# Second MLP of a fused attention and two-MLP kernel: early token sums kept in program order, three plain token quarters split ahead and sent through DRAM

## The chip, the cores and the metric

One core of one Trainium2 chip. The metric is the device time of one execution in microseconds, the median of three runs. Engines are named as the profile names them: PE (TensorE matmul), PEld (its weight load), DVE (VectorE), ACT (ScalarE), POOL (GpSimd), SP (SyncE, whose queue issues all the DMAs of this kernel).

## What is computed

Attention through 32 packed tokens per head, then a gated MLP with an RMS norm, then a second MLP. The change lies in the second MLP alone:

```python
def _moe2_ref(x, w_in, w_out):          # x: 4608 x 512, w_in: 512 x 2048, w_out: 2048 x 512
    h = x @ w_in
    g = h * (1.0 / (1.0 + np.exp(-1.702 * h)))
    return (g @ w_out).astype(np.float32)
```

## The kernel before

Every matrix product is made of three matmuls: an operand is split into a high part (a rounded copy, `fp32r`) and a low part (the value less its high part), and high*high, high*low and low*high are added in PSUM. A split is therefore always a copy on ACT and a subtraction on DVE or POOL.

The second MLP (`mlp2`, `main` in it) multiplies 2x2 blocks with seven products in place of eight. The tokens go through it in five batches, the list `spans`: three of 2 x 512 tokens, two of 2 x 384. The four quarters of a batch's activations are `b11`, `b12`, `b21`, `b22` (half of the tokens by half of the 512 columns; 128 partitions x 2 x 512, or x 2 x 384), and the seven operands that multiply are three plain quarters, `b11`, `b21`, `b22`, and four sums: t1 = b12 - b11, t3 = b22 - b12, t2 = b22 - t1, t4 = b21 - t2. Each lives, split, in one tile of its own (`x_tile`, `x_b...` and `x_t...` in the profile), which the next batch overwrites.

A batch takes four groups of hidden columns (`NGR`), each of 14 up products (`up`, L1065 in the profile: six matmuls; two rounds a = 0, 1 of the seven operands). Beside the ups of one group run the seven down products (`down`, L1136: 24 matmuls of 256 columns, or 18) of the group before, one down after two ups. `form` (L1101 to L1110) makes the down operands: sums on DVE, `oh` on ACT, `ol` on POOL. Weights come from DRAM in the order of use: `wi`, `WIB` ups ahead, `wo`, four downs ahead.

The next batch's quarters are loaded by `load_x` into `xr` tiles (three in the tag `raw`, one in `xr`). `sums` forms t1, t3, t2 in the third and fourth group (table `EARLY`: steps counted from the third group's first up; L1024, L1026, L1030), and after the last use of an operand, in the last seven ups, `prepare` splits the new one into its tile (L1041 on ACT; L1042 on POOL for the plain quarters, on DVE for the sums) and forms t4 (L1045). Nothing ties the early sums to a place: Tile's scheduler orders each engine's instructions by its own estimate of when they are ready, unless `tc.keep_in_program_order` pins one behind what is already written for its engine. An engine runs its instructions in that order, and so does the SP queue.

The four table entries and lines that matter:

```python
EARLY = {10: "t1", 13: "t3", 16: "t2"}            # and load_x at step 6
nc.vector.tensor_sub(xr[q], xr["b12"], xr["b11"])          # sums, t1
(nc.gpsimd if q[0] == "b" else nc.vector).tensor_sub(...)  # prepare, low part
nc.gpsimd.tensor_sub(ol, src, fl(oh))                      # form
```

Of the kernel before, what the change touches and what calls it, by code (L numbers as in the profile page):

```python
# [9 lines left out]
F32 = mybir.dt.float32  # L10
F32R = mybir.dt.float32r
# [15 lines left out]
def fl(t):  # L27

    return t.bitcast(F32)
# [3 lines left out]
def tile_pack_attention__then__two_mlps(  # L33
# [14 lines left out]
    nc = tc.nc  # L48
# [9 lines left out]
    P = 128  # L58
# [30 lines left out]
    TH = 512  # L89
    WHOLE = 3  # L90
    HALF = DM // 2
    spans = [(i * 2 * TH, TH) for i in range(WHOLE)]
# [1 line left out]
        spans.append((spans[-1][0] + 2 * spans[-1][1], (NT - WHOLE * 2 * TH) // 4))  # L94
    SECOND = 3600.0
    SOON = NP2 - 1
    WIB = 11
    WOB = 4
    LAG = 2
    CALM = 2600.0  # L100
# [3 lines left out]
    dram = ctx.enter_context(tc.tile_pool(name="dram", bufs=1, space=DRAM))  # L104
    wi2_d = [dram.tile([P, 7, 2, 2, P], F32, name=f"wi2_{p}") for p in range(NP2)]
    wo2_d = [dram.tile([P, 7, 2, 2, HALF], F32, name=f"wo2_{i}") for i in range(NGR)]
    x2_d = [dram.tile([P, NM, S], F32, name=f"x2_{b}") for b in range(B)]
    wg_d = [dram.tile([P, 2, NPAIR, 2 * P], F32, name=f"wg_{j}") for j in range(NF1)]
    wo_d = [dram.tile([P, 2, DM], F32, name=f"wo_{j}") for j in range(NF1)]

# [720 lines left out]
    def mlp2(cv):  # L831
# [85 lines left out]
        def x_tile(q, n=TH):  # L917
            xb[q] = pools["pre"].tile([P, 2, 2, TH], F32R, tag=q, name=f"x_{q}", bufs=1)[:, :, :, :n]
            return xb[q]
# [4 lines left out]
        def load_part(dst, i0, at0, n):  # L924
            end = at0 + n
            while at0 < end:
                b, s0 = divmod(at0, S)
                m = min(end - at0, S - s0)
                o = at0 + n - end
                nc.sync.dma_start(dst[:, :, o : o + m], x2_d[b][:, i0 : i0 + 2, s0 : s0 + m])  # L930
                at0 += m

        def split_x(q, src, engine, n=TH):
            t = x_tile(q, n)
            nc.scalar.copy(t[:, 0], src)
            engine.tensor_sub(t[:, 1], src, fl(t[:, 0]))

        def first_x():

            t0, n = spans[0]  # L940
# [46 lines left out]
        def main(wp, sp, pm, pa, later):  # L987
            turns = [(s, g) for s in range(len(spans)) for g in range(NGR)]
# [3 lines left out]
            def load_wi(c):  # L992
                if 7 <= c < len(ups):
                    t, a, q = ups[c]
                    wi[c] = wp.tile([P, 2, 2, P], F32R, tag="wi", name="wi", bufs=WIB)
                    nc.sync.dma_start(fl(wi[c]), wi2_d[2 * turns[t][1] + a][:, blocks.index(q)])
# [7 lines left out]
            xr = {}  # L1004

            def load_x(s):
                if s < len(spans):
                    t0, n = spans[s]
                    for q, i0, k in (("b11", 0, 0), ("b12", 0, 1), ("b22", 2, 1), ("b21", 2, 0)):
# [4 lines left out]
                        xr[q] = t[:, :, :n]  # L1014
                        load_part(xr[q], i0, t0 + k * n, n)

            def sums(s, q):

                if s == len(spans):
                    return  # L1020
                n = spans[s][1]
                if q == "t1":
                    xr[q] = wp.tile([P, 2, TH], F32, tag="xt", name="xr", bufs=1)[:, :, :n]
                    nc.vector.tensor_sub(xr[q], xr["b12"], xr["b11"])  # L1024
                elif q == "t3":
                    nc.vector.tensor_sub(xr["b12"], xr["b22"], xr["b12"])  # L1026
                else:
                    xr[q] = [cv.tile([P, TH], F32, tag="w", name="xr", bufs=2)[:, :n] for _ in range(2)]
                    for k in range(2):
                        nc.vector.tensor_sub(xr[q][k], xr["b22"][:, k], xr["t1"][:, k])  # L1030

            def prepare(s, q):

                if s == len(spans):
                    return
                n = spans[s][1]
                src = xr[{"t3": "b12", "t4": "b21"}.get(q, q)]
                t = x_tile(q, n)
                for k in range(2):
                    part = src[k] if q == "t2" else src[:, k]  # L1040
                    nc.scalar.copy(t[:, 0, k], part)  # L1041
                    (nc.gpsimd if q[0] == "b" else nc.vector).tensor_sub(t[:, 1, k], part, fl(t[:, 0, k]))  # L1042
                if q == "b21":
                    for k in range(2):
                        nc.vector.tensor_sub(src[:, k], src[:, k], xr["t2"][k])  # L1045

            g, bank, u2 = {}, {}, {}

# [43 lines left out]
            def form(d):  # L1092

                t, j = divmod(d, 7)
                n = spans[turns[t][0]][1]
                a11, a12, a21, a22 = (g[t, z] for z in ((0, 0), (1, 0), (0, 1), (1, 1)))
                q = down_order[j][0]
                if q == "s2":
                    x = sp.tile([P, 2, TH], F32, tag="s1", name="s1", bufs=1)[:, :, :n]
                    g[t, "s1"] = x  # L1100
                    nc.vector.tensor_add(x, a21, a22)  # L1101
                    nc.vector.tensor_sub(a21, a11, a21)
                    nc.vector.tensor_sub(a11, x, a11)
                elif q == "s4":
                    nc.vector.tensor_sub(a12, a12, a11)
                source = {"a11": a11, "s2": a11, "a12": a12, "s4": a12, "s3": a21, "a22": a22}
                src = g[t, "s1"] if q == "s1" else source[q]
                oh, ol = (sp.tile([P, 2, TH], F32R, tag=f"o{x}", name=f"o{x}", bufs=3)[:, :, :n] for x in "hl")
                nc.scalar.copy(oh, src)  # L1109
                nc.gpsimd.tensor_sub(ol, src, fl(oh))  # L1110
                formed[d] = oh, ol

            acc, banks = {}, {}
# [61 lines left out]

            for c in range(7, WIB + 1):
                load_wi(c)
            for d in range(WOB):
                load_wo(d)
            EARLY = {10: "t1", 13: "t3", 16: "t2"}  # L1180
            form_at, down_at = {}, {}
            for d in range(7 * len(turns)):
                t, j = divmod(d, 7)
# [3 lines left out]
            for c in range(len(ups) + PER + LAG):  # L1187
                if c < len(ups):
                    up(c)
                    load_wi(c + WIB)  # L1190
                    if c >= 7:
                        next(later, None)
                    s, at = turns[ups[c][0]][0], (turns[ups[c][0]][1] - NGR + 2) * PER + c % PER
                    if at == 6:
                        load_x(s + 1)
                    elif at in EARLY:
                        sums(s + 1, EARLY[at])
                for d in form_at.get(c, ()):
                    form(d)
                for d in down_at.get(c, ()):  # L1200
                    down(d)
                    load_wo(d + WOB)
# [4 lines left out]
    with ExitStack():  # L1207
# [8 lines left out]
        cv = ctx.enter_context(tc.tile_pool(name="cv", bufs=1, side="left"))  # L1216
        with ExitStack() as st1:
# [4 lines left out]
            at = st2.enter_context(tc.tile_pool(name="at", bufs=1, side="right"))  # L1222
# [52 lines left out]
            sources = [mm]  # L1275
            between = lambda: sources[-1]
            weights, first_x, first_w, second = mlp2(cv)
            converting, ready = weights(between, range(SOON)), 0.0
            every = EVERY / len(todo)
# [43 lines left out]
        with ExitStack() as st3:  # L1323
            pm = st3.enter_context(tc.tile_pool(name="pm", bufs=1, space=PSUM, side="right"))
            pa = st3.enter_context(tc.tile_pool(name="pa", bufs=1, space=PSUM, side="left"))
            wp = st3.enter_context(tc.tile_pool(name="wp", bufs=1, side="left"))
# [43 lines left out]
```

## Time and profile before

| | us |
|---|---|
| median of three runs (lowest, highest) | 1644.51 (1642.76, 1645.05) |
| the profiled execution, its own time | 1639.52 |
| its span, first to last instruction | 1637.7 |
| of it the second MLP, from its first up | from 898.7 |

The profiled execution is one more run than the three of the median. Its time is 1.8 us more than its span. The batches begin near 899, 1038, 1205, 1369 and 1495 us. In the table of stretches the clock is the mean clock granted to TensorE, 1.00 being 2.4 GHz and 0.50 being 1.2 GHz.

### The profile page before, as it was taken

How to read it: one execution, taken by the hardware profiler on the slowest of the kernel's cores; microseconds unless marked ns; L12 is line 12 of the kernel's file. 1: busy time of each engine (PE TensorE's matmuls, PEld its weight loads, DVE VectorE, ACT ScalarE, POOL GpSimd, SP SyncE). 2: the span in 40 equal slices, each digit the busy share in tenths (PEclk: the TensorE clock that was granted, in tenths of full speed). 3: DMA queues.
4: the chain of work that ended last, by engine and by line, in shares of the span. 5: the costliest groups of instructions: out<-in, count | busy, mean ns of one | idle time of the engine just before them, and what ended most of it. 6: DMA issues, size and time to landing. Idle time of an engine off the chain costs nothing.

```text
span 1637.7 us, 29088 instructions
## 1 busy us (share of the span) xinstructions
PE 1599.6 (98%) x10608; PEld 1514.1 (92%) x10608; DVE 1098.9 (67%) x1895; ACT 872.0 (53%) x1799; POOL 927.6 (57%) x753
## 2 busy tenths in 40 slices
PE   8999999999999999999999999899989999999997
PEld 5699999999999999999999899799979999999997
DVE  5777777767777777676764676844584458567466
ACT  5677777666566665565654544344343434434432
POOL 3547877656665566554655475554455445646444
PEclk9999999999999999999999999999999999999999
DMA  9756665866546655484544996576657667887874
GB/s 263 220 170 190 212 203 193 275 198 213 202 161 217 194 170 169 158 309 148 176 172 174 317 326 195 189 242 190 182 189 237 192 191 225 284 252 247 285 232 141
DMA packets 217725, 348.21 MB, mean 213 GB/s; under 512 B 93936, under 2 KB 123632, under 8 KB 211440
## 3 DMA queue, kind: packets, MB, share of 16 engines
q1 hardware_dynamic: 217584, 346.35, 66.0%
q8 instruction: 85, 1.39, 0.4%
q14 instruction: 56, 0.46, 0.1%
HBM read 279.19 MB, written 67.11 MB: 211 GB/s over the span
## 4 chain that ended last, share of the span: by engine, by line
PE 90%; DVE 5%; issue 1%; DMA 1%; ACT 1%; POOL 0%; SPq 0%; POOLq 0%; DVEq 0%; ACTq 0%
PE ps_dn L1136 20%; PE ps_up L1065 19%; PE ps_o L748 19%; PE ps_g L712 18%; PE ps_w L679 4%; PE ps_at L308 3%; PE ps_at L297 3%; PE ps_at L353 2%; PE ps_at L443 2%; DVE xr L1030 1%; PE ps_at L341 1%; DVE x_t L1042 1%; DMA xr<-x 1%; DVE xr L1045 0%; PE ps_at L281 0%
## 5 line engine op out<-in xcount | busy, mean ns | idle before, releaser
L1110 POOL TENSOR_TENSOR ol<-g,oh 128x1024 fp32r<-128x1024 f32 (+1 forms) x120 | 269.4, 2255 | 301.0 <-ACT oh L1109 300.1
L1136 PE MATMUL ps_dn<-wo,oh 128*128 128x256 f32 x2016 | 368.8, 284 | 9.7 <-DVE accu L1163 5.8
L1136 PEld LDWEIGHTS ps_dn<-wo,oh 128*128 128x128 f32 x2016 | 320.5, 192 | 17.4 <-DVE accu L1163 6.2
L748 PE MATMUL ps_o<-Hh,wo 128*128 128x384 f32 x1152 | 320.3, 340 | 0.1
L1136 PE MATMUL ps_dn<-wo,ol 128*128 128x256 f32 x1008 | 280.7, 284 | 1.0 <-POOL ol L1110 1.0
L712 PE MATMUL ps_g<-Aqh,Wh 128*128 128x288 f32 x768 | 231.7, 302 | 3.8 <-DVE th L722 2.7
L712 PE MATMUL ps_g<-Aql,Wh 128*128 128x288 f32 x768 | 226.2, 295 | 0.0
L712 PE MATMUL ps_g<-Aqh,Wl 128*128 128x288 f32 x768 | 226.0, 295 | 0.0
L734 POOL TENSOR_TENSOR Hl<-th,Hh 128x576 fp32r<-128x576 f32 x96 | 138.2, 1440 | 138.0 <-ACT Hh L733 137.8
L1065 PE MATMUL ps_up<-x_t,wi 128*128 128x512 f32 (+1 forms) x936 | 213.4, 368 | 1.1 <-DVE g L1087 1.1
L748 PEld LDWEIGHTS ps_o<-Hh,wo 128*128 128x128 f32 x1152 | 209.9, 188 | 2.1 <-DVE th L725 0.3
L1088 ACT ACTIVATE g<-g 128x512 f32<-128x512 f32 (+1 forms) x120 | 70.6, 590 | 237.5 <-DVE g L1085 130.7
L748 PE MATMUL ps_o<-Hl,wo 128*128 128x384 f32 x576 | 194.2, 337 | 0.0
L1136 PEld LDWEIGHTS ps_dn<-wo,ol 128*128 128x128 f32 x1008 | 191.5, 192 | 2.2 <-POOL ol L1110 1.6
L684 DVE TENSOR_TENSOR Wl<-ps_w,Wh 64x512 fp32r<-64x512 f32 x192 | 131.8, 687 | 81.9 <-ACT Wh L683 78.7
L1065 PEld LDWEIGHTS ps_up<-x_t,wi 128*128 128x128 f32 x936 | 166.3, 188 | 20.9 <-DVE g L1087 1.9
L1065 PE MATMUL ps_up<-x_b,wi 128*128 128x512 f32 (+1 forms) x702 | 165.5, 371 | 5.3 <-DVE g L1080 5.3
L763 POOL TENSOR_TENSOR acc<-acc,add 128x384 f32<-128x384 f32 x135 | 138.6, 1038 | 50.2 <-ACT add L761 48.6
L1109 ACT CAST oh<-g 128x1024 fp32r<-128x1024 f32 (+1 forms) x120 | 113.3, 961 | 94.7 <-PE ps_dn L1136 65.5
L683 ACT CAST Wh<-ps_w 64x512 fp32r<-64x512 f32 x192 | 111.5, 581 | 81.9 <-PE ps_w L679 50.7
L712 PEld LDWEIGHTS ps_g<-Aqh,Wh 128*128 128x128 f32 x768 | 144.2, 188 | 7.7 <-DVE th L722 3.2
L1163 DVE TENSOR_TENSOR acc<-acc,ps_dn 128x512 f32<-128x512 f32 (+1 forms) x160 | 99.6, 630 | 72.3 <-PE ps_dn L1136 68.0
(201 smaller groups left out, 3267.5 us busy)
## 6 DMA issues: line engine op xcount, KB each, us to landing
wo<-wo SPq DMA_DIRECT2D x188, 512.0 KB, 3.9
wi<-wi SPq DMA_DIRECT2D x274, 256.0 KB, 3.7
wg<-wg SPq DMA_DIRECT2D x48, 1024.0 KB, 6.4
raw<-in_moe_w_out_dram SPq DMA_DIRECT2D x28, 512.0 KB, 4.6
wi<-stage SPq DMA_DIRECT2D x24, 512.0 KB, 4.0
wo<-stage SPq DMA_DIRECT2D x24, 512.0 KB, 3.6
x<-acc SPq DMA_DIRECT2D x32, 288.0 KB, 3.3
vn<-in_v_dram SPq DMA_DIRECT2D x16, 512.0 KB, 6.9
```

The costliest lines, as they stand in the source:

```text
L683: nc.scalar.copy(Wh[rows, :, g], src)
L684: nc.vector.tensor_sub(Wl[rows, :, g], src, fl(Wh[rows, :, g]))
L712: nc.tensor.matmul(ps, st[:, o, g, c * P : (c + 1) * P], mv[:, g, cols], start=n == 0, stop=n == 3 * NG - 1)
L734: nc.gpsimd.tensor_sub(Hl, th, fl(Hh))
L748: nc.tensor.matmul(ps, st[:, m * P : (m + 1) * P], mv[:, cols], start=n == 0, stop=n == 3 * len(ss) - 1)
L763: nc.gpsimd.tensor_add(a, a, t)
L1065: nc.tensor.matmul(o, w[:, y, k], x[:, z, k], start=i == 0 and not go_on, stop=i == 5, skip_group_check=bool(go_on))
L1088: nc.scalar.activation(gf, o if q == "a12" else gf, AF.Gelu_apprx_sigmoid)
L1109: nc.scalar.copy(oh, src)
L1110: nc.gpsimd.tensor_sub(ol, src, fl(oh))
L1136: nc.tensor.matmul(o[:, r], x[:, a, (r0 + r) * P : (r0 + r + 1) * P], w[:, a, y], start=i == 0 and not go_on, stop=i == 6 * m - 1, skip_gr ...
L1163: nc.vector.tensor_add(z, z, o[:, :m])
```

## The change

- The x loads of the next batch are written at step 2 of the third group instead of 6 (`load_x`).
- t1, t3, t2 and now t4 too are one DVE subtraction each, in place of one of their sources, pinned; `prepare` no longer forms t4.
- The plain quarters are split early, at steps 8, 9 (b11), 13, 14 (b22), 17, 18 (b21), half a quarter a step, into a new tile `part` (two buffers): copy on ACT, subtraction on DVE, pinned. The split half is stored to new DRAM tiles `x2s`, 512 KB (384 KB in the smaller batches).
- In `prepare` a plain quarter is now one load from `x2s` into its tile (1 MB, or 768 KB), with no compute.
- `WIB` is 10 instead of 11.
- In the last group of the last batch the `ol` subtractions of the last four down operands go to DVE instead of POOL.

```diff
-    WIB = 11
+    WIB = 10
...
+    x2s_d = [{q: dram.tile([P, 2, 2, n], F32, name=f"x2s_{s}{q}") for q in ("b11", "b22", "b21")} for s, (_, n) in enumerate(spans)]
...
             def sums(s, q):
...
-                if q == "t1":
-                    xr[q] = wp.tile([P, 2, TH], F32, tag="xt", name="xr", bufs=1)[:, :, :n]
-                    nc.vector.tensor_sub(xr[q], xr["b12"], xr["b11"])
-                elif q == "t3":
-                    nc.vector.tensor_sub(xr["b12"], xr["b22"], xr["b12"])
-                else:
-                    xr[q] = [cv.tile([P, TH], F32, tag="w", name="xr", bufs=2)[:, :n] for _ in range(2)]
-                    for k in range(2):
-                        nc.vector.tensor_sub(xr[q][k], xr["b22"][:, k], xr["t1"][:, k])
+                if q in ("t1", "t2", "t3", "t4"):
+                    x, y, home = {
+                        "t1": ("b12", "b11", "b11"), "t3": ("b22", "b12", "b12"),
+                        "t2": ("b22", "b11", "b22"), "t4": ("b21", "b22", "b21"),
+                    }[q]
+                    pinned(nc.vector.tensor_sub(xr[home], xr[x], xr[y]))
+                    return
+                q, k = q.split(".")
+                src = xr[q][:, int(k)]
+                t = wp.tile([P, 2, TH], F32R, tag="part", name="part", bufs=2)[:, :, :n]
+                nc.scalar.copy(t[:, 0], src)
+                pinned(nc.vector.tensor_sub(t[:, 1], src, fl(t[:, 0])))
+                nc.sync.dma_start(x2s_d[s][q][:, :, int(k)], fl(t))
...
             def prepare(s, q):
...
-                src = xr[{"t3": "b12", "t4": "b21"}.get(q, q)]
                 t = x_tile(q, n)
+                if q[0] == "b":
+                    nc.sync.dma_start(fl(t), x2s_d[s][q])
+                    return
+                src = xr[{"t1": "b11", "t2": "b22", "t3": "b12", "t4": "b21"}[q]]
                 for k in range(2):
...
-                    (nc.gpsimd if q[0] == "b" else nc.vector).tensor_sub(t[:, 1, k], part, fl(t[:, 0, k]))
-                if q == "b21":
-                    for k in range(2):
-                        nc.vector.tensor_sub(src[:, k], src[:, k], xr["t2"][k])
+                    nc.vector.tensor_sub(t[:, 1, k], src[:, k], fl(t[:, 0, k]))
...
-                nc.gpsimd.tensor_sub(ol, src, fl(oh))
+                late = t == len(turns) - 1 and j >= 3
+                (nc.vector if late else nc.gpsimd).tensor_sub(ol, src, fl(oh))
...
-            EARLY = {10: "t1", 13: "t3", 16: "t2"}
+            EARLY = {8: "b11.0", 9: "b11.1", 10: "t1", 12: "t3", 13: "b22.0", 14: "b22.1", 15: "t2", 17: "b21.0", 18: "b21.1", 19: "t4"}
...
-                    if at == 6:
+                    if at == 2:
```

Up to the second MLP the order of every engine is the same in both programs. In it, three places matter. The first is DVE where the third batch has just begun (TensorE is at its first ups). Before:

```order
L1103 TENSOR_TENSOR g<-s_15020,g 128x1024
L1163 TENSOR_TENSOR accu<-accu,ps_dn 128x512
L1026 TENSOR_TENSOR xr<-xr 128x2x384
L1030 TENSOR_TENSOR xr<-xr 128x384 x2
L1163 TENSOR_TENSOR accu<-accu,ps_dn 128x512
L1078 TENSOR_TENSOR u_15067<-u_15067,ps_up 128x512
L1080 TENSOR_TENSOR g<-u_15067,ps_up 128x512
```

and with the change:

```order
L1105 TENSOR_TENSOR g<-s_15053,g 128x1024
L1166 TENSOR_TENSOR accu<-accu,ps_dn 128x512 x2
L1080 TENSOR_TENSOR u_15100<-u_15100,ps_up 128x512
L1082 TENSOR_TENSOR g<-u_15100,ps_up 128x512
L1087 TENSOR_TENSOR g<-g,ps_up 128x512
```

Before, the sums t3 and t2 of the fourth batch (their 384 tells it) stand here, a whole batch ahead of their place in the program; with the change none stands here, nor at the start of any other batch.

The second place is the start of a batch's fourth group (here of the second batch), where the new work now stands. ACT with the change (`part_14681` is the second half of b22, `part_14755` and `part_14798` are b21; `oh_14634` is the second down operand of the group):

```order
L1078 COPY u2_14677<-ps_up_14666 128x512
L1031 CAST part_14755<-xr_14335 128x512
L1031 CAST part_14798<-xr_14335 128x512
L1111 CAST oh_14634<-g_14264 128x1024
L1111 CAST oh_14685<-g_14266 128x1024
```

and DVE there:

```order
L1103 TENSOR_TENSOR s1_14630<-g_14265,g_14267 128x1024
L1166 TENSOR_TENSOR acc2_13926<-acc2_13926,ps_dn_14522 128x2x256
L1166 TENSOR_TENSOR acc2_13926<-acc2_13926,ps_dn_14523 128x2x256
L1032 TENSOR_TENSOR part_14681<-xr_14332,part_14681 128x512
L1104 TENSOR_TENSOR g_14265<-g_14264,g_14265 128x1024
L1026 TENSOR_TENSOR xr_14332<-xr_14332,xr_14326 128x1024
L1105 TENSOR_TENSOR g_14264<-s1_14630,g_14264 128x1024
```

On ACT two copies of b21 have moved ahead of the two `oh` copies; on DVE one half of b22 and the sum t2 (L1026) have moved in between the sums of `form` (L1103 to L1105). TensorE's order holds one more up product ahead of the second down product there.

The third place is the SP queue at the end of the second batch:

```order
L1033 DMA x2s_2b21_85<-part_14798 256x1x512
L998 DMA wo2_14843<-wo2_2_67 128x1024
L992 DMA wi_14871<-wi2_0_57 128x512
L931 DMA xr_15934<-x2_5_74 128x2x384
L1042 DMA x_b11_14867<-x2s_2b11_83 128x2048
L992 DMA wi_14915<-wi2_0_57 128x512
```

The load of the split b11 (`x_b11`) stands behind the last store of a split half and behind the first raw load for the batch after next (`xr_15934`).

## Rows read from the trace of the kernel before

**Rows 1.** the page: engine totals, then the chain that ended last by engine

```profile
PE 1599.6 (98%) x10608; PEld 1514.1 (92%) x10608; DVE 1098.9 (67%) x1895; ACT 872.0 (53%) x1799; POOL 927.6 (57%) x753
...
PE 90%; DVE 5%; issue 1%; DMA 1%; ACT 1%; POOL 0%; SPq 0%; POOLq 0%; DVEq 0%; ACTq 0%
```

**Rows 2.** windows: stretch, its us, busy us per engine, clock, DMA share, GB/s

```profile
1040.00:1060.00 20.00, 14.15 (x81) 12.44 (x80) 18.63 (x18) 5.18 (x7) 8.72 (x4) 0.84 0.58 197
1200.00:1220.00 20.00, 14.57 (x89) 12.76 (x88) 19.47 (x18) 6.36 (x9) 12.79 (x6) 0.94 0.54 194
1220.00:1240.00 20.00, 20.00 (x122) 18.61 (x122) 10.32 (x15) 5.63 (x7) 14.93 (x7) 0.89 0.48 145
1360.00:1380.00 20.00, 18.43 (x125) 17.57 (x124) 18.76 (x25) 9.38 (x15) 9.35 (x6) 1.00 0.77 249
1480.00:1500.00 20.00, 20.00 (x144) 20.00 (x143) 17.90 (x27) 10.17 (x22) 10.74 (x8) 1.00 0.79 243
1500.00:1520.00 20.00, 20.00 (x145) 20.00 (x144) 12.57 (x21) 8.71 (x14) 17.42 (x10) 1.00 0.81 256
```

**Rows 3.** timeline, DVE, 1212 to 1219 us: start, us, instruction, idle before

```profile
1212.24 0.96 DVE L1026 TENSOR_TENSOR xr<-xr 128x768 f32<-128x768 f32 x1 [0.39 <-DMA xr<-x]
1213.11 5.34 DVE L1030 TENSOR_TENSOR xr<-xr 128x384 f32<-128x384 f32 x2
1218.37 0.67 DVE L1163 TENSOR_TENSOR accu<-accu,ps_dn 128x512 f32<-128x512 f32 x1
```

**Rows 4.** timeline, TensorE, 1213 to 1230 us

```profile
1219.10 0.80 PE L1136 MATMUL ps_dn<-wo,oh 128*128 128x256 f32 x2 [5.04 <-DVE accu L1163]
...
1219.91 0.63 PE L1136 MATMUL ps_dn<-wo,oh 128*128 128x256 f32 x2
...
1227.91 1.54 PE L1065 MATMUL ps_up<-x_t,wi 128*128 128x512 f32 x6
```

**Rows 5.** timeline, ACT: copies of the first up bank, five of them

```profile
1017.79 0.58 ACT L1076 COPY u<-ps_up 128x512 f32<-128x512 f32 x1
...
1065.15 0.59 ACT L1076 COPY u<-ps_up 128x512 f32<-128x512 f32 x1
...
1104.52 0.59 ACT L1076 COPY u<-ps_up 128x512 f32<-128x512 f32 x1
...
1143.86 0.59 ACT L1076 COPY u<-ps_up 128x512 f32<-128x512 f32 x1
...
1230.85 0.59 ACT L1076 COPY u<-ps_up 128x512 f32<-128x512 f32 x1
```

**Rows 6.** instruction groups of the second MLP, and one DVE pair

```profile
L1110 POOL TENSOR_TENSOR ol<-g,oh 128x1024 fp32r<-128x1024 f32 x72 | 177.9, 2480 | 199.5 <-ACT oh L1109 199.5
...
L1042 DVE TENSOR_TENSOR x_t<-xr,x_t 128x512 fp32r<-128x512 f32 x16 | 12.8, 842 | 2.7 <-ACT x_t L1041 2.7
...
1191.23 1.28 DVE L1042 TENSOR_TENSOR x_t<-xr,x_t 128x512 fp32r<-128x512 f32 x2
```

**Rows 7.** timeline, 1164 to 1172 us: DVE, ACT, TensorE in the fourth group

```profile
1164.79 1.22 DVE L1103 TENSOR_TENSOR g<-s,g 128x1024 f32<-128x1024 f32 x1
...
1166.05 2.00 ACT L1109 CAST oh<-g 128x1024 fp32r<-128x1024 f32 x2 [0.48 <-DVE g L1103]
...
1171.76 0.64 PE L1136 MATMUL ps_dn<-wo,oh 128*128 128x256 f32 x4
```

**Rows 8.** DMA issues: count, KB, us to landing (second MLP; whole kernel)

```profile
wi<-stage SPq DMA_DIRECT2D x3, 512.0 KB, 4.4
...
wi<-stage SPq DMA_DIRECT2D x1, 256.0 KB, 6.2
...
wg<-wg SPq DMA_DIRECT2D x48, 1024.0 KB, 6.4
```

**Rows 9.** timeline, TensorE, the last 25 us

```profile
1615.73 1.47 PE L1136 MATMUL ps_dn<-wo,oh 128*128 128x256 f32 x8 [0.89 <-ACT oh L1109]
...
1627.40 0.50 PE L1136 MATMUL ps_dn<-wo,oh 128*128 128x256 f32 x2 [1.41 <-DVE acc L1163]
```

More of the change, by code (lines that the diff above doesn't have):

```diff
@@ L931, in load_part @@
                 at0 += m
[L933 to L936, printed above, removed]
         def first_x():
@@ L1015, in load_x, with pinned @@
                         load_part(xr[q], i0, t0 + k * n, n)
+            def pinned(i):
+                tc.keep_in_program_order(i)
             def sums(s, q):
@@ L1036, in prepare @@
                 n = spans[s][1]
-                src = xr[{"t3": "b12", "t4": "b21"}.get(q, q)]
                 t = x_tile(q, n)
+                if q[0] == "b":
+                    nc.sync.dma_start(fl(t), x2s_d[s][q])
+                    return
+                src = xr[{"t1": "b11", "t2": "b22", "t3": "b12", "t4": "b21"}[q]]
                 for k in range(2):
-                    part = src[k] if q == "t2" else src[:, k]
-                    nc.scalar.copy(t[:, 0, k], part)
-                    (nc.gpsimd if q[0] == "b" else nc.vector).tensor_sub(t[:, 1, k], part, fl(t[:, 0, k]))
-                if q == "b21":
-                    for k in range(2):
-                        nc.vector.tensor_sub(src[:, k], src[:, k], xr["t2"][k])
+                    nc.scalar.copy(t[:, 0, k], src[:, k])
+                    nc.vector.tensor_sub(t[:, 1, k], src[:, k], fl(t[:, 0, k]))
             g, bank, u2 = {}, {}, {}
```

## The prediction

> **What bounds the kernel now.** I read the page's totals and its chain first: TensorE is busy 98% of the span, and the chain that ended last is 90% TensorE and 5% DVE [rows 1]. So nothing is won by faster work elsewhere; what is to be had is the time in which TensorE waits or runs at its lower clock. The stretches of the second MLP show where that is: TensorE is idle for 20 - 14.15 = 5.85 us near 1050, 5.43 us near 1210 and 1.57 us near 1370 [rows 2]. These are the starts of the second, third and fourth batch. The start of the fifth, in the two stretches from 1480 to 1520, has none: 20.00 of 20 twice [rows 2]. The fifth batch's start has the same splits as the others; what it has not is early sums, since no sixth batch follows.
>
> The timeline of DVE at the third batch shows the wait itself [rows 3]. The sums t3 and t2 of the batch after (384 columns) stand there; t3 first waits 0.39 us for a load, then it and the two halves of t2 hold DVE from 1212.24 to 1218.4, and only then comes the `accu` addition that empties a PSUM bank. TensorE waits 5.04 us for just that addition [rows 4]. After the wait it is also slow: pairs of 256-column matmuls take 0.63 us where six of 512 columns take 1.54 us a little later [rows 4], and the granted clock of the stretch behind falls to 0.89, at the second batch to 0.84 [rows 2], so for some microseconds it had the lower level, 1.2 GHz.
>
> What a start loses in all, idle and clock, is read from the copies of the first up bank, one per half group [rows 5]. Undisturbed, a group takes 1143.86 - 1104.52 = 39.34 us. From 1143.86 to 1230.85 lie two groups: 86.99 - 78.68 = 8.3 us lost. From 1017.79 to 1065.15 lies one: 47.36 - 39.34 = 8.0 us lost. At the fourth batch the clock stays at 1.00, so I take the idle time alone, 1.6 us. Together 17.9 us.
>
> **The change part by part.** *Early sums, pinned.* In the new order none of them stands at a batch's start; DVE goes from the `form` sums straight to `accu` and the up banks. The cause of all three waits is removed: -17.9 us. They now run in the third and fourth group, spread over some 60 us; over the whole span DVE is busy 67% [rows 1].
>
> *The plain quarters' splits.* 24 subtractions go from POOL to DVE, six per batch, and their copies on ACT move forward with them. One costs DVE 0.64 us where it runs undisturbed (1.28 for a pair) and 0.84 us in the mean [rows 6]: 6 x 0.84 = 5 us in two groups of 39.34, beside TensorE. DVE is in order, so what counts is who stands behind. At the fourth group's start two things move in front of the second down operand. On DVE half of b22 (0.64) and t2 (as large as L1103, 1.22) delay the last `form` sum from 1164.79 [rows 7] by about 1.9 us, and the first half of b22 by 0.6 more. On ACT two copies of b21 stand in front of the two `oh` casts, and the second needs the buffer of b22's second half, which is free only when its store has landed. That half is split some 0.3 us after 1164.8; a store of 512 KB lands in 4.4 us [rows 8], so at 1169.5; the copy takes some 0.6 and the first `oh` cast 1.0 (2.00 for two [rows 7]): 1171.1. Before, TensorE took up that product at 1171.76 [rows 7]; in the new order one more up product stands ahead of it (six matmuls, 1.4 us): 1173.1. So 2 us are left, and the hidden work costs nothing; with the slowest store in the rows, 6.2 us [rows 8], 0.2 us are left. If that cover goes, TensorE waits for the excess. Bounds for the four starts together: 0 and, with every store 2 us slower than the slowest row, 4 x 1.8 = 7 us. I take 1 us, near the lower end, since the median store leaves slack.
>
> *The price of a subtraction on DVE.* The two halves of t2 took 2.67 us each [rows 3] and the pair of x_t 0.64 each [rows 6], for fewer elements in the former; POOL's `ol` takes 2.48 us [rows 6], and DVE's time in rows 3 is like waiting for two of those. By the rows the moved subtractions cost 0.64 to 2.67 us each. The Trainium skill, SBUF — State Buffer, Who interferes with whom, says that a DVE instruction with two SBUF inputs and a GpSimd instruction that reads SBUF exclude each other for a whole instruction; rows 3 agree, 2.67 us being far over 0.64. By that rule the sum would hold up to 2.5 us for each moved subtraction that meets an `ol`, and the second rival would be the forecast.
>
> *The way through DRAM.* 24 stores and 12 loads come onto the SP queue. A load of 1 MB lands in 6.4 us [rows 8]. It is issued once the last up on the old tile is done, and the next batch reads b11 seven ups and four downs later, at least half a group, some 19 us; so 13 us are left and nothing is lost. It waits behind a raw load and the last store of a half; both are ready some microseconds earlier. Behind a store that waits for DVE stand weight loads, but those run ten ups ahead, some 28 us. For the same reason one `wi` tile less costs nothing. DMA is at 0.48 to 0.81 of its engines there [rows 2]; two more transfers of at most 12 x 1 MB each way lie inside that.
>
> *The last operands' `ol` on DVE.* TensorE's last 25 us hold waits of 0.89 and 1.41 us among others [rows 9]. One `ol` on DVE is shorter than on POOL, but DVE is also what TensorE waits for at 1627.40 [rows 9]. Bounds: a gain of the 2.3 us, or a loss as large. I take 0.
>
> **The sum.** -8.0 - 8.3 - 1.6 + 1 + 0 = -16.9 us on the profiled execution's 1639.52: 1622.6. That execution is 5.0 us under the median of 1644.51, so against the median I forecast 1644.5 - 17 = **1627.5 us**. With the bounds of the unknown terms (7 for 1, and 2.3 each way at the end) the likeliest case spans 1624 to 1636.
>
> **The rivals.** *Half is given back.* DVE in the fourth group meets `ol` on POOL with two or three of its moved instructions and TensorE waits some 2 us at each of the four starts, too short to lose the clock. Price 4 x 2 = 8: 1635. For it: DVE was already busy 17.9 of 20 us over the end of the fourth batch [rows 2]. Against: at that place TensorE lost nothing. 0.15.
>
> *DVE and POOL exclude each other (slower).* The place is the fourth group of each batch: of the moved subtractions and sums there, five meet an `ol` and each waits 2.5 us, 12.5 us, less some 2 us of slack, and behind a wait that long TensorE also gets the lower clock, about 2.9 us as at the third batch (8.3 - 5.43). That is 13 us four times, 52 - 17.9 = +34: 1679 at worst. It decides from 4.5 us of wait a start on, where the four eat up 17.9; at 6 us with the clock's share of 1.5 it would give 1657. Against: a half group, some 20 us [rows 5], holds only three or four `ol` of 2.48 us [rows 6], so POOL is idle half of the time. 0.06. The rule of the skill named above is the mechanism of this one.
>
> *No change.* The early sums are gone, but what is late next is the new load or the store that ACT waits for: a store that lands 4.5 us after the 6.2 of the rows, at each start, gives the 17.9 back: 1644. Against: the two landing rows, 4.4 and 6.2. 0.06. That the change does not do what it says is out: the new order shows the sums moved.
>
> *More than forecast.* The end gains its 2.3 us and the starts cost nothing: 1644.5 - 17.9 - 2.3 = 1624; the small waits ahead of the starts may go as well: 1623. 0.13.
>
> **How the numbers follow.** The forecast has 0.60, half given back 0.15, more than forecast 0.13, no change 0.06, slower 0.06. A difference under 0.2% (3.3 us) can't be told from none here. Faster is 0.60 + 0.15 + 0.13 = 0.88, same 0.06, slower 0.06. The range, 1621 to 1638, holds the first three with their bounds and leaves out the last two.
>
> **What would show it.** Right: at the starts of batches two to four TensorE is busy 20 of 20 us at clock 1.00, the first-bank copies stand 39.3 us apart across them, no `xr` subtraction lies between `form` and `accu` there, and the `x_b` loads land over 10 us ahead of their ups. Wrong: TensorE waiting for `oh` or `ol` in a fourth group, ACT idle on a DMA ahead of its b21 copies, DVE subtractions of 2.5 us in a row there, or a clock under 1.00 at new places.

## The result, and the profile after

The changed kernel takes **1621.62 us** (median of four runs, 1619.16 to 1622.48) against 1643.63 before (four runs too, 1641.84 to 1645.05): a ratio of 0.9864, 95% interval 0.9847 to 0.9881. That is 22.0 us less. 1627.5 was forecast; the time lies at the lower end of the range of 1621 to 1638. The profiled execution takes 1620.81 us with a span of 1619.0, 18.7 less than the 1637.7 of before.

The page of the changed kernel, engine totals and chain, answers to [rows 1]. TensorE's busy time fell by 6.7 us and DVE's share of the chain from 5% to 2%; DVE itself is as busy as before.

```profile
PE 1592.9 (98%) x10608; PEld 1509.3 (93%) x10608; DVE 1103.5 (68%) x1915; ACT 869.3 (54%) x1799; POOL 886.0 (55%) x725
...
PE 90%; DMA 2%; DVE 2%; ACT 2%; issue 2%; POOL 1%; SPq 1%; POOLq 0%; ACTq 0%; DVEq 0%
```

The windows of the changed kernel around the starts of batches 2 to 4, with the columns of [rows 2]. TensorE is busy 20.00 of 20 us at a granted clock of 1.00 in every one, where before had 14.15, 14.57 and 18.43, and a clock of 0.84 and 0.94 at the first two.

```profile
1040.00:1060.00 20.00, 20.00 (x130) 18.24 (x129) 13.01 (x15) 8.10 (x11) 14.25 (x7) 1.00 0.91 316
1180.00:1200.00 20.00, 20.00 (x131) 18.27 (x131) 17.30 (x26) 9.69 (x17) 7.40 (x3) 1.00 0.97 357
1200.00:1220.00 20.00, 20.00 (x128) 18.14 (x127) 11.89 (x14) 8.91 (x11) 16.68 (x8) 1.00 0.83 287
1360.00:1380.00 20.00, 20.00 (x148) 20.00 (x147) 10.65 (x14) 7.39 (x13) 17.65 (x8) 1.00 0.79 255
```

DVE's timeline at the third batch's start in the changed kernel answers to [rows 3]. Between the last `form` sum (L1105 now) and `accu` (L1166) no `xr` subtraction is left, and it is DVE that waits for TensorE.

```profile
1198.60 1.21 DVE L1105 TENSOR_TENSOR g<-s,g 128x1024 f32<-128x1024 f32 x1
1199.74 0.67 DVE L1166 TENSOR_TENSOR accu<-accu,ps_dn 128x512 f32<-128x512 f32 x1
1201.15 0.69 DVE L1166 TENSOR_TENSOR accu<-accu,ps_dn 128x512 f32<-128x512 f32 x1 [0.74 <-PE ps_dn L1139]
```

The copies of the first up bank in the changed kernel (ACT; L1078 now), of the first half of each group from batch 2 to 3, answer to [rows 5]. They stand 39.35 us apart straight across the third batch's start at 1196.92.

```profile
1118.21 0.59 ACT L1078 COPY u<-ps_up 128x512 f32<-128x512 f32 x1 [0.80 <-PE ps_up L1067]
...
1157.56 0.59 ACT L1078 COPY u<-ps_up 128x512 f32<-128x512 f32 x1 [1.90 <-PE ps_up L1067]
...
1196.92 0.59 ACT L1078 COPY u<-ps_up 128x512 f32<-128x512 f32 x1 [2.41 <-PE ps_up L1067]
...
1236.27 0.59 ACT L1078 COPY u<-ps_up 128x512 f32<-128x512 f32 x1 [2.90 <-PE ps_up L1067]
```

The same copies tell where the time came from. The table has the times at which five of them start in the profiles of four kernels (the second and third kernel are experiments, told below):

| first-half copy | before | before, second profile | sums held alone | changed |
|---|---|---|---|---|
| batch 1, first group | 903.80 | 904.58 | 902.51 | 903.78 |
| batch 1, fourth group | 998.50 | 999.27 | 997.58 | 1000.14 |
| batch 2, second group | 1086.28 | 1087.64 | 1076.28 | 1078.85 |
| batch 3, second group | 1251.97 | 1254.97 | 1233.68 | 1236.27 |
| batch 5, second group | 1524.86 | 1527.68 | 1504.59 | 1507.17 |
| end of the span | 1637.7 | 1640.5 | 1617.5 | 1619.0 |

From row to row, before against changed: +1.6 in batch 1, -9.1 at the start of batch 2, -8.3 at that of batch 3, -2.0 over the starts of batches 4 and 5, -1.0 at the end; in all -18.7.

TensorE waits nowhere from 1035 to 1590 in this profile. How near it comes to a wait is seen in the fourth group of batch 2 (timeline of the changed kernel, DVE, SP, ACT and TensorE), which answers to [rows 7].

```profile
1157.85 0.68 DVE L1032 TENSOR_TENSOR part<-xr,part 128x512 fp32r<-128x512 f32 x1
...
1158.59 0.52 SPq L1033 DMA_DIRECT2D x2s_2b<-part  x1
...
1160.73 1.21 DVE L1105 TENSOR_TENSOR g<-s,g 128x1024 f32<-128x1024 f32 x1
...
1163.15 0.62 ACT L1031 CAST part<-xr 128x512 fp32r<-128x512 f32 x1 [3.29 <-DVE accu L1166]
1163.67 2.00 ACT L1111 CAST oh<-g 128x1024 fp32r<-128x1024 f32 x2
...
1165.70 0.64 PE L1139 MATMUL ps_dn<-wo,oh 128*128 128x256 f32 x4
...
1165.37 2.39 DVE L1032 TENSOR_TENSOR part<-xr,part 128x512 fp32r<-128x512 f32 x1
1168.41 2.16 DVE L1047 TENSOR_TENSOR x_t<-xr,x_t 128x512 fp32r<-128x512 f32 x1 [0.65 <-ACT x_t L1046]
1170.49 3.42 DVE L1107 TENSOR_TENSOR g<-g 128x1024 f32<-128x1024 f32 x1
```

ACT's second b21 copy starts at 1163.15. The store issued at 1158.59, whose buffer it needs, lands 4.5 us later, at 1163.1. The idle time is put down to a DVE `accu`, which has nothing to do with that buffer, so I read it as the landing. The first `oh` is then ready at 1164.7, and TensorE takes it up at 1165.70: 1.0 us of slack.

DMA issues of the changed kernel (count, KB, median us to landing), the answer to [rows 8]:

```profile
x2s_2b<-part SPq DMA_DIRECT2D x6, 512.0 KB, 4.2
x_b<-x2s_2b SPq DMA_DIRECT2D x3, 1024.0 KB, 7.4
```

TensorE's waits in the last 25 us of the changed kernel, the answer to [rows 9]. Before, it waited 0.89 for `oh`, 0.43 for POOL's `ol`, 0.77 for `accu` and 1.41 for `acc`. The last two are gone; a second wait for `ol` and one of issue (in which it waited for nothing that the profile shows) have come.

```profile
1598.04 1.47 PE L1139 MATMUL ps_dn<-wo,oh 128*128 128x256 f32 x8 [0.89 <-ACT oh L1111]
1599.95 0.39 PE L1139 MATMUL ps_dn<-wo,ol 128*128 128x256 f32 x1 [0.43 <-POOL ol L1113]
1602.46 0.39 PE L1139 MATMUL ps_dn<-wo,ol 128*128 128x256 f32 x1 [0.57 <-POOL ol L1113]
1612.10 0.48 PE L1139 MATMUL ps_dn<-wo,oh 128*128 128x256 f32 x2 [0.88 <-issue]
```

### The profile page after: what moved, and what is told of

It is laid out like the page before. It is cut to its first block, busy times and chain, and to the rows that moved or that the text cites. A ratio compares the mean times of both kernels' runs of the same rounds, so it can differ in the third digit from the quotient of the medians.

```text
span 1619.0 us, 29164 instructions
## 1 busy us (share of the span) xinstructions
PE 1592.9 (98%) x10608; PEld 1509.3 (93%) x10608; DVE 1103.5 (68%) x1915; ACT 869.3 (54%) x1799; POOL 886.0 (55%) x725
## 4 chain that ended last, share of the span: by engine, by line
PE 90%; DMA 2%; DVE 2%; ACT 2%; issue 2%; POOL 1%; SPq 1%; POOLq 0%; ACTq 0%; DVEq 0%
PE ps_dn L1139 20%; PE ps_o L749 19%; PE ps_up L1067 18%; PE ps_g L713 18%; PE ps_w L680 4%; PE ps_at L309 3%; PE ps_at L298 2%; PE ps_at L354 2%; PE ps_at L444 2%; DMA wi<-wi 1%; PE ps_at L342 1%; POOL ol L1113 1%; DMA raw<-in_moe_w_in_dram 0%; DMA raw<-in_moe_w_out_dram 0%; DMA kw<-in_k_dram 0%
## 5 line engine op out<-in xcount | busy, mean ns | idle before, releaser
L1113 POOL TENSOR_TENSOR ol<-g,oh 128x1024 fp32r<-128x1024 f32 (+1 forms) x117 | 260.3, 2236 | 344.7 <-ACT oh L1111 315.9
L713 PEld LDWEIGHTS ps_g<-Aql,Wh 128*128 128x128 f32 x768 | 144.3, 188 | 0.3 <-DVE Aql L697 0.2
```

Source lines behind the costliest of these rows:

```text
L713: nc.tensor.matmul(ps, st[:, o, g, c * P : (c + 1) * P], mv[:, g, cols], start=n == 0, stop=n == 3 * NG - 1)
L1113: (nc.vector if late else nc.gpsimd).tensor_sub(ol, src, fl(oh))
```

## The experiments

The theory: the gain is that DVE no longer has early sums ahead of `accu` at a start. The rivals: the way through DRAM and the moved splits are part of it; the waits were for loads and for POOL, not for the sums; the end is worth nothing. Twelve runs:

| run | what it is | median us | range | ratio to before, 95% |
|---|---|---|---|---|
| before_again | before, again | 1642.31 | 1640.40 to 1645.81 | 0.9993 to 1.0014 |
| e1_pin_alone | before, sums held | 1620.66 | 1619.51 to 1621.31 | 0.9852 to 0.9882 |
| e9_pin_t2 | before, only t2 held | 1630.37 | 1629.93 to 1631.48 | 0.9910 to 0.9937 |
| e2_no_pin | change, nothing held | 1628.44 | 1627.86 to 1629.36 | 0.9900 to 0.9930 |
| e6_one_part | change, one `part` buffer | 1622.08 | 1620.37 to 1623.60 | 0.9860 to 0.9892 |
| e3_end_on_pool | change, end on POOL | 1623.55 | 1622.02 to 1624.22 | 0.9863 to 0.9895 |
| after_again | the change, again | 1622.76 | 1621.69 to 1623.81 | 0.9865 to 0.9892 |
| e8_pin_and_end | sums held, end as changed | 1620.30 | 1620.08 to 1621.03 | 0.9846 to 0.9876 |
| e8_again | the same | 1619.60 | 1619.33 to 1620.55 | 0.9847 to 0.9874 |
| e12_one_wi_less | the same, `WIB` = 10 | 1621.15 | 1620.55 to 1624.57 | 0.9859 to 0.9892 |
| e10_pin_and_end_more | sums held, six `ol` on DVE | 1619.84 | 1618.24 to 1623.95 | 0.9841 to 0.9879 |
| e10_again | the same | 1618.50 | 1616.69 to 1619.20 | 0.9837 to 0.9864 |

**The sums alone.** The three kinds of sums of the kernel before, wrapped, and nothing else:

```diff
-                    nc.vector.tensor_sub(xr[q], xr["b12"], xr["b11"])
+                    tc.keep_in_program_order(nc.vector.tensor_sub(xr[q], xr["b12"], xr["b11"]))
...
-                    nc.vector.tensor_sub(xr["b12"], xr["b22"], xr["b12"])
+                    tc.keep_in_program_order(nc.vector.tensor_sub(xr["b12"], xr["b22"], xr["b12"]))
...
-                        nc.vector.tensor_sub(xr[q][k], xr["b22"][:, k], xr["t1"][:, k])
+                        tc.keep_in_program_order(nc.vector.tensor_sub(xr[q][k], xr["b22"][:, k], xr["t1"][:, k]))
```

> The kernel before with the sums t1, t3 and t2 held to their place in the program and nothing else: the splits of the plain quarters stay at the end of the batch on ACT and POOL, nothing goes through DRAM. Theory A (the whole gain is that DVE no longer has sums ahead of accu at a start): the waits of 5.29, 5.04 and 1.57 us go, 17 us less than before, 1624 to 1628 us, within 4 us of the changed kernel. Rival B (moving the splits off the start and through DRAM is needed too, since POOL's six subtractions there delay ol): half of it, some 1635 us, with TensorE waiting for ol of POOL at the starts.

Measured 1620.66: the whole gain. The windows of this kernel show TensorE without a gap at the starts, while DVE is as good as full ahead of one and POOL still makes its splits there.

```profile
1040.00:1060.00 20.00, 20.00 (x128) 18.13 (x127) 14.34 (x17) 8.85 (x11) 13.68 (x6) 1.00 0.70 224
1180.00:1200.00 20.00, 20.00 (x130) 18.23 (x130) 19.90 (x23) 8.61 (x16) 9.78 (x6) 1.00 0.72 235
```

So the order of the sums is enough, and rival B falls: neither the splits' move nor the way through DRAM is needed for it.

**The change without holding.** `pinned` returns its instruction and does nothing else:

```diff
             def pinned(i):
-                tc.keep_in_program_order(i)
+                return i
```

> The changed kernel with its sums and splits left to the scheduler, everything else as it is (way through DRAM, buffers, turns). Its order brings sums and splits of the batch after next back to the starts. Theory A (holding them to the order of the program is what pays): waits for accu or for form come back at the starts of batches 2 to 4, 10 to 20 us more than the changed kernel, 1632 to 1642 us. Rival B (the way through DRAM pays, wherever the sums stand): within 2 us of the changed kernel, 1620 to 1624 us.

Measured 1628.44, 6 to 7 us more than the change: between the two expectations. By the copies of the up bank, 3.1 us go from the middle of batch 1's third group over the start of batch 2, 3.5 at the start of batch 4, and nothing at that of batch 3. Its windows:

```profile
1000.00:1020.00 20.00, 18.80 (x120) 16.75 (x120) 17.02 (x18) 6.82 (x9) 11.70 (x5) 1.00 0.79 250
1040.00:1060.00 20.00, 19.21 (x119) 17.19 (x119) 19.69 (x22) 9.35 (x14) 9.25 (x4) 1.00 1.04 393
1360.00:1380.00 20.00, 17.42 (x122) 16.57 (x121) 15.44 (x20) 8.98 (x14) 10.65 (x5) 1.00 0.98 351
```

Waits come back, but short ones, of 0.8 to 1.5 us, and the clock stays at 1.00. So something else in the change does part of the work even without holding. Which part (the earlier turns, the sums made in place or the splits' new way) no run separates.

**A dose.** Only the two halves of t2 are held, so that t1 and t3 stay ahead:

```diff
-                        nc.vector.tensor_sub(xr[q][k], xr["b22"][:, k], xr["t1"][:, k])
+                        tc.keep_in_program_order(nc.vector.tensor_sub(xr[q][k], xr["b22"][:, k], xr["t1"][:, k]))
```

> The kernel before with only the two halves of t2 held to their place: at the starts t1 and t3 stay ahead of accu, the 5.3 us of t2 go. It is the dose between the kernel before and the one with all sums held. Theory A (TensorE's wait is DVE's time in front of accu, less a slack, and the low clock follows only a long wait): the waits of 5.3, 5.0 and 1.6 us fall to 0 to 2 us, the clock stays at 1.00, 1621 to 1626 us. Rival B (what DVE waits for at the start is the load of xr and POOL, not the sums' own time): waits of 3 us or more and a clock under 1.00 stay there, 1630 to 1640 us.

Measured 1630.37, and neither expectation holds in full. The window of this kernel at the start of batch 2, and DVE and TensorE in its timeline at the starts of batches 2 and 3:

```profile
1040.00:1060.00 20.00, 17.08 (x104) 14.89 (x103) 17.74 (x20) 6.83 (x9) 10.42 (x5) 1.00 0.59 208
...
1051.11 1.60 DVE L1026 TENSOR_TENSOR xr<-xr 128x1024 f32<-128x1024 f32 x1 [1.85 <-DMA xr<-x]
1053.37 1.65 PE L1065 MATMUL ps_up<-x_t,wi 128*128 128x512 f32 x6 [2.25 <-DVE u L1078]
...
1210.66 2.41 DVE L1026 TENSOR_TENSOR xr<-xr 128x768 f32<-128x768 f32 x1 [1.36 <-DMA xr<-x]
1213.72 0.50 PE L1136 MATMUL ps_dn<-wo,oh 128*128 128x256 f32 x2 [2.22 <-DVE accu L1163]
```

The clock stays at 1.00, as theory A has it, and TensorE's waits at these places fall to 2.2 us, just over its bound of 2; the time lies in rival B's range. What t3 still costs is its own time and the up to 1.85 us that DVE stands for its load before it. By the copies the three starts lose 3.5, 3.5 and 1.0 us, against 9.1, 8.3 and 2.0 with all sums left free and nothing with all held: a sum that is not ready costs an in-order engine its wait as well as its own time.

**Before, again.** No edit.

> The kernel before, unchanged, for a second profile and more timed runs. If the profiled execution of 1639.52 us was one of the quick ones by chance, a second one lies nearer to the timed median, 1641 to 1645, and the first copies of the up banks of the second MLP stand as far apart as in the first profile (47.4 us where batch 2 starts, 39.3 us undisturbed): the 3 us would then lie ahead of the second MLP. If they are instead part of what the change saves, one of the starts loses more than 8.3 us here.

It was partly the one and partly the other. The second profile takes 1642.31 us, nearer to the median. The third batch's start loses 9.9 us in it instead of 8.3, by the table of copies. DVE in the second profile of before:

```profile
1214.03 2.95 DVE L1026 TENSOR_TENSOR xr<-xr 128x768 f32<-128x768 f32 x1 [0.82 <-DMA xr<-x]
1216.90 5.30 DVE L1030 TENSOR_TENSOR xr<-xr 128x384 f32<-128x384 f32 x2
1222.13 0.67 DVE L1163 TENSOR_TENSOR accu<-accu,ps_dn 128x512 f32<-128x512 f32 x1
```

Measured from the end of DVE's `accu` before it, the load came 0.4 us later; t3 took 2.95 us instead of 0.96, and TensorE waited 7.42 us instead of 5.04. With batch 2 (9.7 for 9.1) and batch 4 (1.8 for 2.0) this execution loses 2.0 us more at the starts, of the 2.8 by which its span is longer; the other 0.8 lie ahead of the second MLP. The first profile of before, 1639.52, was a quick one.

**The end.** With the sums held and `ol` of the last operands on DVE, four of them and six of them:

```diff
-                nc.gpsimd.tensor_sub(ol, src, fl(oh))
+                late = t == len(turns) - 1 and j >= 3
+                (nc.vector if late else nc.gpsimd).tensor_sub(ol, src, fl(oh))
```

> The kernel before with the sums held to their place in the program and, as in the change, ol of the last four operands on DVE; nothing through DRAM. In the profiles the stretch from the last copy of the up bank to the end of the span is 38.8 us in the changed kernel and 39.9 us with the sums held alone. Theory A (the end gains 1 us by ol on DVE, whatever else): 1.0 us less than with the sums held alone, 1619.7 us, and faster than the changed kernel by 1 to 2 us. Rival B (the shorter end comes from what else the change moved): no difference to the kernel with the sums held alone, 1620.7 us.

> The kernel before with the sums held and ol of the last four operands on DVE, again: 1620.3 us as in its first runs (1619.5 to 1621.5).

> The same with ol of the last six operands on DVE instead of four. TensorE's two short waits for ol of POOL ahead of them (0.4 to 0.6 us each) should go; DVE, for which TensorE waits in the end of the kernel before (0.8 and 1.4 us), gets 2 to 2.5 us more work. Theory A (POOL's ol is late there, DVE is not): 0.4 to 1 us less than with four, 1618.7 to 1619.3 us. Rival B (DVE is the later one): the same as with four or up to 1.5 us more.

> The same with ol of the last six operands on DVE, again. In the profiles the end is 37.5 us from the last copy of the up bank, against 38.6 us with four and 39.9 us with none. Theory A (that is the gain): 1 us less than with four, 1619.3 us. Rival B (lost in what differs from execution to execution ahead of the second MLP): no difference that the runs can tell.

And the changed kernel with `late = False`:

> The changed kernel with ol of the last operands back on POOL. It differs from the kernel with the sums held alone by the way through DRAM and the earlier splits only. Theory A (the end's ol is worth 1 us, the way through DRAM nothing): 1 us more than the changed kernel, 1622 to 1623 us, with TensorE waiting for acc and accu of DVE at the end as before. Rival B (the end's ol is worth nothing): the same as the changed kernel.

From the last first-bank copy to the end of the span lie 39.8 us before, 39.9 with the sums held, 39.95 with the change and `late = False`; 38.8 in the change, 38.6 and 38.7 with four `ol` on DVE, 37.5 and 37.45 with six (in the six, `j >= 1`). The waits of TensorE after 1590 in the change with `late = False` are those of before again:

```profile
PE ps_dn L1139 <- DVE acc L1166: 1.4, 1, 1.4
...
PE ps_dn L1139 <- DVE accu L1166: 0.8, 1, 0.8
```

So the end is worth 1.0 to 1.3 us with four and 2.4 with six, where the two waits for POOL's `ol` go too. By these stretches theory A holds for all three. The medians agree in sign each time (0.4 and 1.1 us with four, 0.5 and 1.1 more with six, 1.9 and 0.8 for the two medians of the change), but they scatter about theory A's figures by up to 0.8 us, and in single runs the gain drowns in other differences. Timeline of TensorE's waits at the end of the kernel with six, second run:

```profile
1596.71 1.48 PE L1137 MATMUL ps_dn<-wo,oh 128*128 128x256 f32 x8 [0.89 <-ACT oh L1109]
1606.29 0.47 PE L1137 MATMUL ps_dn<-wo,oh 128*128 128x256 f32 x2 [0.42 <-issue]
1609.55 0.47 PE L1137 MATMUL ps_dn<-wo,oh 128*128 128x256 f32 x2 [0.89 <-issue]
```

This is the fastest kernel of the study: the kernel before with the sums held and six `ol` on DVE, 1619.84 and 1618.50 us in its two runs, beside 1621.62 and 1622.76 of the change.

**One `part` buffer.** `bufs=2` becomes `bufs=1`.

> The changed kernel with one buffer instead of two for the split halves on their way to DRAM, so that every split waits until the store of the one before has landed (4.0 to 4.4 us after its issue in the profile of the changed kernel), on ACT ahead of oh in the fourth group. It tests the slack of 1 to 2 us that the prediction gave to the first oh there. Theory A (the landing is close to the path, as the sum says): the cast that waits is ahead of an oh, so oh comes 2 to 5 us late once per start, 1 to 4 us of it wait of TensorE: 5 to 16 us more over the four starts, 1626 to 1638 us. Rival (there is far more slack than the sum says): within 2 us of the changed kernel.

Measured 1622.08, as the change. With one buffer the scheduler set ACT's b21 copy behind the `oh` casts, so that only the second half of b22 waits ahead of them; in batch 2 for 0.42 us. In the fourth group of batch 4 it is longer. Timeline of this kernel, SP, ACT, DVE and TensorE:

```profile
1446.10 0.52 SPq L1033 DMA_DIRECT2D x2s_4b<-part  x1
...
1451.56 0.51 ACT L1031 CAST part<-xr 128x384 fp32r<-128x384 f32 x1 [3.48 <-DMA x2s_4b<-part]
...
1452.10 0.56 DVE L1032 TENSOR_TENSOR part<-xr,part 128x384 fp32r<-128x384 f32 x1 [2.31 <-ACT part L1031]
...
1455.93 0.50 PE L1139 MATMUL ps_dn<-wo,oh 128*128 128x256 f32 x2 [1.34 <-DVE accu L1166]
```

The store lands, ACT's copy waits 3.48 us for it, DVE's split waits 2.31 for the copy, t2 comes behind it and `accu` is late: TensorE waits 1.34 us, and by the copies this fourth group loses 1.9 us. So the wait that the prediction priced is real, through DVE's order rather than through `oh`; with half the buffers it costs 1.9 us at one of four starts, far under the 5 to 16 of theory A. With two buffers ACT waits 2.13 us for a landing at the same place, and TensorE for nothing.

**What the way through DRAM costs.** The changed kernel beside the sums and the end alone, and that one with ten `wi` tiles as in the change:

> The changed kernel, unchanged, on one chip with the two below, to tell whether the way through DRAM costs or gains anything beside the sums held to their place. So far its median is 1621.6 us against 1620.3 with the sums held and the end on DVE. Theory A (the way through DRAM is worth nothing: from the second batch on the copies of the up bank stand equally far apart in both): within 1 us of the next kernel here. Rival B (it costs 1 to 3 us, as the medians so far hint): 1 to 3 us more than the next one.

> The kernel with the sums held and ol of the last four operands on DVE, with ten wi tiles instead of eleven, as the change has them to make room for its split halves; nothing through DRAM. In the second execution of the changed kernel TensorE waits 0.6 us for a wi load at the start of batch 5, and ACT waits up to 7 us for a weight load in batch 1; the changed kernel stands 1.3 and 3.2 us above the kernel with sums and end alone. Theory A (the tile less is what costs them): 1621 to 1623 us, as the changed kernel. Rival B (the loads and stores of the way through DRAM cost it, or nothing does): 1619.5 to 1620.5 us, as with eleven.

Eight runs of the change have a median of 1622.2 us, eight with sums and end alone 1620.1: 2.1 us or 0.13%, under what the measurement can tell for certain, but of one sign in both pairs. From batch 2's second group to batch 5's the first profile of the change and the kernel with the sums alone agree to 0.01 us (1507.17 - 1078.85 = 428.32, 1504.59 - 1076.28 = 428.31), so nothing of it is lost there. In the second profile of the change batch 5's start loses 0.8 us, behind this wait of TensorE:

```profile
PE ps_up L1067 <- DMA wi<-wi: 0.6, 1, 0.6
```

And in batch 1 ACT stands 7.06 us for a weight load in it, where it stood 4.65 before, and TensorE then waits 1.8 us for `oh` and `ol`:

```profile
952.16 0.67 ACT L130 ACTIVATE w<-raw 128x512 f32<-128x512 f32 x1 [7.06 <-DMA raw<-in_moe_w_out_dram]
```

Such a wait in batch 1 appears in executions without the way through DRAM too (6.40 us for the load and 1.3 of TensorE in the first run of sums and end), so it is not the change's own. The change's first store of a split half is issued only after these waits of TensorE (at 985.90, and at 983.69 in the first profile), so the transfers of the way through DRAM did not cause them. With sums, end and ten `wi` tiles the kernel takes 1621.15, just inside theory A's range, but its four runs, 1620.55 to 1624.57, overlap those of both neighbours, and in its profile TensorE waits nowhere from 990 to 1590. So a tile less is not shown to cost anything, and where the 2 us between the medians come from stays open.

## Why the prediction was right, and where it was off

**The cause** was read rightly from [rows 2 to 4]: held sums alone give the gain, and not holding gives 6 to 7 us of it back. That batch 5 had no wait because no sums follow it was the comparison that pointed to it ahead of any run.

**The starts** were put at 8.0, 8.3 and 1.6, and are worth 9.1, 8.3 and 2.0 in the profile pair. The term of batch 2 was mis-sized: it was read from the copies at 1017.79 and 1065.15 [rows 5], and the first of them, a group's second half, stands where the scheduler puts it; the same stretch has 38.5 us in the changed kernel, not 39.34. Copies of first halves stand 39.35 apart and are the better ruler. At batch 4 the idle time of 1.57 missed 0.4.

**New waits in the fourth groups** were put at +1 with bounds of 0 and 7, and are 0. The chain of steps came out as written, each step a little late: the last `form` sum 3.4 us later than before (1.9 and 0.6 put), the first `oh` ready 1.0 ahead of TensorE (2 put), TensorE's take-up at 1165.70 where 1173.1 less the 7.4 already saved puts it. Two of the signs named for being wrong do stand there: ACT idle on a store ahead of its b21 copies (3.29 us for the second), and DVE subtractions of 2.39, 2.16 and 3.42 us in a row. But nothing that TensorE waits for stands behind them. The Trainium skill, SBUF — State Buffer, Who interferes with whom, says that a DVE instruction with two SBUF inputs and a GpSimd instruction that reads SBUF shut each other out. The traces agree: 3.42 us for a sum beside POOL's `ol` (1169.98 to 1172.83), against 1.21 for one of the same size. In the fourth groups this price fell beside the path.

At the starts of the kernel before it lay on the path. Two rows of before, at the start of batch 4:

```profile
1374.98 1.02 DVE L1030 TENSOR_TENSOR xr<-xr 128x384 f32<-128x384 f32 x2
...
1378.29 4.77 POOL L1110 TENSOR_TENSOR ol<-g,oh 128x1024 fp32r<-128x1024 f32 x2 [9.41 <-ACT oh L1109]
```

Here POOL is idle, and the two halves of t2 take 1.02 us. At batch 3 the same two take 5.34 [rows 3], beside POOL's `ol`. TensorE's waits are 1.57 and 5.04 us. By these rows a start lost as much as it did through the order and POOL's `ol` together. That is read from the rows alone: no run moves the `ol` away from a start, and holding the order takes the whole wait away.

That the profiles' sum still holds some +1 for new waits is chance. In the pair it is 1.6 us in batch 1, in a stretch of old weight loads that the prediction had not looked at. Between first and fourth group that stretch takes 94.7 us in both profiles of before and 96.4 in the first profile of the change, but also 96.4 and 94.7 in the two profiles of the kernel with sums and end alone.

**The way through DRAM** was put at nothing with 13 us left. The load of batch 3's b11 is issued at 1180.82 and lands 6.4 us later, as put, and TensorE's first product with it, ahead of the copy at 1196.92, begins at 1195.33. From issue to use are 14.5 us instead of the 19 put, so 8.1 us are left and the mark of "over 10 us" was missed, without cost. The other two loads there take 7.4 and 11.4 us. That one `wi` tile less costs nothing was not refuted: in one of the change's two profiles TensorE waits 0.6 us for a `wi` load, but in the other, and in that of sums and end with ten tiles, it does not.

**The price of a subtraction on DVE**, 0.84 put, is 0.96 us in the mean for 512 tokens.

**The end** was put at 0 with bounds of 2.3 each way, and is -1.0. DVE gets the work and still is less in the way. The prediction weighed the `ol` on the two engines; what stands on DVE ahead of the `acc` that TensorE waited for are two additions of `acc` and `accu`, and these became shorter. DVE in the kernel before, in the change, and in the change with `late = False`:

```profile
1622.85 4.17 DVE L1167 TENSOR_TENSOR acc<-acc,accu 128x768 f32<-128x768 f32 x2
...
1605.11 1.82 DVE L1170 TENSOR_TENSOR acc<-acc,accu 128x768 f32<-128x768 f32 x2
...
1607.44 4.18 DVE L1170 TENSOR_TENSOR acc<-acc,accu 128x768 f32<-128x768 f32 x2
```

Where they take 4.17 and 4.18 us, three `ol` run on POOL beside them for 7.58; in the change these `ol` are on DVE, 0.95 us each.

**The sum and the median.** -16.9 were put and -18.7 measured between the profiles: -1.1 from batch 2, -0.4 from batch 4, -1.0 at the end, +0.6 for new waits. The other 3.3 of the 22.0 are between profiles and medians: the saving was taken from an execution of before that ran quicker than the timed runs beside it. The second profile of before puts 2.0 us of such a difference down to the starts. That the quantity to be removed differs from execution to execution was in none of the bounds. The time is thus nearest to the rival *more than forecast*, which had 0.13: 1.4 us below its 1623, and 2.4 below the likeliest case's own 1624 to 1636. It is inside the stated range by 0.6 us. The other three rivals fell.

## What to carry to other kernels

Work that can run early but is needed late is worth holding in place on an in-order engine that the bound engine waits for: left free, it stood here just ahead of an urgent instruction, and the load that it waited for then stood in front of everything. Before building a detour to lighten such a place, hold the order alone and measure: here three wrapped calls gave all that the detour through DRAM gave. And where a wait depends on a transfer's landing, take its price from more than one execution.

## What was not expected of the hardware

The cost of the same sum in the same place varied threefold between two executions of one kernel: t3 took 0.96 us in [rows 3] and 2.95 in the second profile of before. POOL in the first and in the second profile:

```profile
1212.41 5.63 POOL L1110 TENSOR_TENSOR ol<-g,oh 128x1024 fp32r<-128x1024 f32 x2 [7.21 <-ACT oh L1109]
...
1213.77 5.41 POOL L1110 TENSOR_TENSOR ol<-g,oh 128x1024 fp32r<-128x1024 f32 x2 [7.21 <-ACT oh L1109]
```

In the first, t3 starts at 1212.24, 0.17 us ahead of POOL's first `ol`, and is done in 0.96. In the second, its load comes 0.4 us later, so it starts at 1214.03, 0.26 us behind the `ol`, and takes 2 us longer. That the late start is the cause is read from these rows; no run sets it apart.

The end shows the same with an edit: with the last `ol` moved off POOL, two additions on DVE that the edit did not touch fell from 4.18 to 1.82 us.
